# A searched instruction order, a halved first segment and LN transposes on TensorE, in a transformer block with segmented attention

## The chip, the core and the metric

The kernel runs on one core of one Trainium2 chip. The metric is device time in microseconds for one launch. The runs of one kernel spread over 1 to 1.5%, so each kernel ran several times, turn by turn with the kernel before on the same chip.

Engine names in the profile: PE is the matmul engine, PEld its weight loads (they overlap matmuls), DVE is VectorE, ACT is ScalarE, POOL is GpSimd, SP the engine that issues most DMAs.

## The reference

One transformer block on 2048 tokens of width 640, bf16: a LayerNorm, an attention in four segments of 512 tokens with 32 heads of 20, its output projection, a residual, a second LayerNorm, and a SiLU feed-forward (FFN) of width 1728. Within a segment the attention is a causal softmax; between segments it reads a memory that the earlier segments filled.

```python
q, k, v = LN(x) @ wq, LN(x) @ wk, LN(x) @ wv          # 32 heads x 20, segments of L = 512
phi = lambda t: where(t > 0, t + 1, exp(t))
M = z = 0
for s in range(4):
    p = softmax(qs @ ks.T * 20**-0.5 + causal_mask)    # within the segment
    o = g * (phi(qs) @ M) / (phi(qs) @ z + 1e-6) + (1 - g) * (p @ vs)
    M, z = M + phi(ks).T @ vs, z + sum(phi(ks))        # g = sigmoid(beta), per head
h = x + o @ wo
out = h + silu(LN(h) @ w1) @ w2
```

## The kernel before

The kernel is written as a graph of some 1,350 tasks. A task is a group of instructions for one engine: ten V matmuls of one token block, one exponential, one cast. At build time a list scheduler plays the graph through with costs in microseconds: whenever an engine is free it starts the ready task of best priority that finds its buffers free. The order that comes out is the order of the instructions on each engine. On the chip each engine works through its list in order and waits on semaphores.

```python
    def schedule(self):
        ...
        while left:
            for e in ENGS:
                if engfree[e] > now + 1e-9: continue
                best = None
                for i in cand[e]:
                    t = tasks[i]
                    if t.start is not None or t.ready > now + 1e-9: continue
                    pr = t.prio
                    if e == AC and DV in t.engs and engfree[DV] <= now + self.flex: continue
                    ...
                    if best is not None and (pr, t.idx) >= best[0]: continue
                    if not can(t): continue                # its buffers are not free
                    best = ((pr, t.idx), t)
                if best is None and e == PE and fill_ok(now):
                    ...                                    # a filler matmul on zeros
```

When PE has nothing to do and its window has been quiet, the scheduler puts in a filler: a matmul on zeros, meant to keep the granted PE clock up.

Four parts of the graph matter here.

```python
    # start: x in four loads, then wq, wk; wv waits for the LN of block 1
    for b in range(4): load_x(b, 1, -100 + b)
    load_w("q", ...); load_w("k", ...)
    load_w("wv", ..., after=lnt(1))

    # every LayerNorm ends in a DMA transpose: tokens x features -> features x tokens
    dma(f"{tag}tr{b}", [(xn, [0])], [(dstA, [i])],
        lambda e: e.dma_start_transpose(out=dst[:, :, 128*i:128*i+128], in_=xn_rot[:, xn.slot, :]), ...)

    # scores of one head group (4 heads): three tiles of key blocks over all 512 queries,
    # then the exponentials on ACT, the causal mask on POOL, P @ V on PE
    for pi, (pool, pt, js, width, cost) in enumerate((
            ("PTA", PTA, [(0, 0)], 512, ...),              # key block 0
            ("PTB", PTB, [(1, 0), (3, 384)], 512, ...),    # key blocks 1 and 3
            ("PTE", PTE, [(2, 0)], 256, ...))):            # key block 2
        ...

    # FFN of a segment: 14 row blocks over all 512 tokens
    h1: matmul(bank(ps)[0:fw, :], lhsT=w1_sb[...], rhs=hT[:, c, :])      # waits for four LN blocks
    th: th = tanh(0.5 * h1)     on ACT
    s : sT = (th + 1) * h1      on DVE
    h2: matmul over sT and w2, then x + 0.5 * h2
```

PSUM has eight banks: four for the score tiles (`sc`), four for everything else (`ps`).

The softmax here doesn't subtract the row's maximum and nothing guards it: scores larger than these inputs give would overflow.

Of the kernel before, what the change touches and what calls it, by code (L numbers as in the profile page):

```python
# [5 lines left out]
ACT = mybir.ActivationFunctionType  # L6
# [226 lines left out]
LAT = {PE: 0.125, AC: 0.16, DV: 0.14, PO: 0.09, SP: 0.0}  # L233


class Graph:
    def __init__(self, pools):
        self.pools = pools
        self.tasks = []
        self.turns = {}  # L240
        self.flex = P["flex"]
        self.filler = None
        self.fill_from = 1.0
        self.fill_to = 1e9
        self.free_order = ("x", "ps", "ex", "th", "st", "xn", "pK", "rd")
# [7 lines left out]
    def task(self, name, engs, emit, reads=(), writes=(), prio=0.0, mode=None, reserve=(), lat=None, bw=0.0):  # L253

        t = Task()
        t.name, t.engs, t.emit, t.prio, t.mode, t.lat, t.bw = name, engs, emit, prio, mode, lat, bw
# [21 lines left out]
        for a in [a for a, _ in t.reads + t.writes] + list(reserve):  # L278
            if a not in al:
                al.append(a)  # L280
# [7 lines left out]
    def schedule(self):  # L288
        import heapq
        tasks = self.tasks  # L290
        for t in tasks:
            t.succ = []
            t.npred = len(t.preds)
            t.ready = 0.0
            t.start = t.eng = None
        for t in tasks:
            for p in t.preds:
                tasks[p].succ.append(t.idx)
        free = {p: [True] * n for p, n in self.pools.items()}
        events = []  # L300
        engfree = {e: 0.0 for e in ENGS}
        pemode = [None]
        WIN = 3.4133
        busy = {}
        rate = {0: 0.5}

        def pe_rate(t):
            w = int(t / WIN)
            for v in range(max(rate), w):
                rate[v + 1] = 1.0 if busy.get(v, 0.0) >= 0.39 * WIN else 0.5  # L310
            return rate[w]

        def pe_busy(st, en, r):
            w = int(st / WIN)
            while st < en:
                e2 = min(en, (w + 1) * WIN)
                busy[w] = busy.get(w, 0.0) + (e2 - st) * r
                st = e2
                w += 1
        dmaq = [0.0]  # L320
        cand = {e: [] for e in ENGS}
        order = []
        left = len(tasks)

        def push(t):
            for e in t.engs:
                cand[e].append(t.idx)

        turn = {p: 0 for p in self.pools}

        def find(a):
            f = free[a.pool]
            if a.pool not in self.free_order and a.turn != turn[a.pool]:
                return None
            if a.size == 1:
                if a.pool == "ps":
                    n = len(f)
                    for i in range(n):
                        if f[i] and not f[i ^ 1]:
                            return i  # L340
                for i, x in enumerate(f):
                    if x:
                        return i
                return None
            for i in range(0, len(f), a.size):
                if all(f[i:i + a.size]):
                    return i
            return None

        def can(t):  # L350
            need = [a for a in t.allocs if a.slot is None]
            if not need:
                return True
            taken = []
            ok = True
            for a in need:
                i = find(a)
                if i is None:
                    ok = False
                    break  # L360
                for k in range(a.size):
                    free[a.pool][i + k] = False
                taken.append((a, i))
            for a, i in taken:
                for k in range(a.size):
                    free[a.pool][i + k] = True
            return ok

        def fill_ok(t):
            return t > self.fill_from and busy.get(int(t / WIN), 0.0) < 0.55 * WIN and t < self.fill_to  # L370

        now = 0.0
        for t in tasks:
            if t.npred == 0:
                push(t)
        done_heap = []
        rel_heap = []
        while left:
            progressed = True
            while progressed:  # L380
                progressed = False
                for e in ENGS:
                    if engfree[e] > now + 1e-9:
                        continue
                    best = None
                    for i in cand[e]:
                        t = tasks[i]
                        if t.start is not None or t.ready > now + 1e-9:
                            continue
                        pr = t.prio  # L390
                        if e == AC and DV in t.engs and engfree[DV] <= now + self.flex:
                            continue
                        if e == PE and pemode[0] is not None and t.mode != pemode[0]:
                            pr += P["mode"]
                        if best is not None and (pr, t.idx) >= best[0]:
                            continue
                        if not can(t):
                            continue
                        best = ((pr, t.idx), t)
                    if best is None and e == PE and self.filler is not None and fill_ok(now):  # L400
                        a = Alloc("ps", 1)
                        if find(a) is not None:
                            t = Task()
                            t.name, t.engs, t.prio, t.mode, t.lat, t.bw = "fill", {PE: 0.107}, 1e9, "f", None, 0.0
                            t.reads, t.writes, t.allocs, t.preds, t.succ, t.npred = [], [(a, [0])], [a], set(), [], 0
                            t.ready, t.start, t.eng = now, None, None
                            t.idx = len(tasks)
                            t.emit = self.filler(a)
                            a.users = 1
                            tasks.append(t)  # L410
                            cand[PE].append(t.idx)
                            left += 1
                            best = ((0, 0), t)
                    if best is None:
                        continue
                    t = best[1]
                    progressed = True
                    for a in t.allocs:
                        if a.slot is None:
                            i = find(a)  # L420
                            a.slot = i
                            turn[a.pool] += 1
                            for k in range(a.size):
                                free[a.pool][i + k] = False
                    cost = t.engs[e]
                    st = now
                    if e == PE and pemode[0] is not None and t.mode != pemode[0]:
                        st += 0.10
                    if e == PE:
                        pemode[0] = t.mode  # L430
                        r = pe_rate(st)
                        cost = cost / r
                        pe_busy(st, st + cost, r)
                    t.start, t.eng = st, e
                    if e == SP:

                        engfree[e] = st + cost
                        b = max(st + (0.9 if t.mode == "tr" else 0.3), dmaq[0])
                        dmaq[0] = b + t.bw
                        end = b + t.bw + 1.5  # L440
                        avail = end
                    else:
                        end = st + cost
                        engfree[e] = end
                        avail = end + (LAT[e] if t.lat is None else t.lat)
                    t.end = end
                    cand[e].remove(t.idx)
                    for e2 in t.engs:
                        if e2 != e:
                            cand[e2].remove(t.idx)  # L450
                    order.append(t)
                    left -= 1
                    heapq.heappush(done_heap, (avail, t.idx))
            nxt = [engfree[e] for e in ENGS if engfree[e] > now + 1e-9]
            nxt += [tasks[i].ready for e in ENGS for i in cand[e] if tasks[i].ready > now + 1e-9]
            if done_heap:
                nxt.append(done_heap[0][0])
# [779 lines left out]
```

## Time and profile before

| | before |
|---|---|
| median of the runs beside the changed kernel | 351.04 us (348.51 to 353.0, 4 runs) |
| profiled span | 346.4 us |
| first V matmul / first score exponential | 15.5 / 23.95 us |
| first FFN matmul | 104.4 us |
| filler matmuls | 62 before the first V matmul, 72 later |

From the profile page of before: the busy time and share of each engine, and the shares of the chain that ended last (followed back from the last instruction, at each step to what released it).

```profile
PE 320.3 (92%) x2750; PEld 165.1 (48%) x2750; DVE 239.6 (69%) x482; ACT 203.8 (59%) x258; POOL 145.5 (42%) x282
...
PE 67%; DVE 15%; ACT 7%; DMA 6%; issue 2%; SPq 1%; POOL 0%; ACTq 0%; DVEq 0%
```

PE is named first in both, but 92% busy does not mean 92% used. The Trainium skill ("Perfetto Trace Analysis", Identifying the Most-Contended Engine) says that matmul busy time is a poor measure because matmuls are pipelined. The trace agrees: a single 512-column matmul is listed at about 380 ns, yet five of them take 1.08 us in the chain, which is 2,370 columns per us. So this document counts columns: the columns of all matmuls at a round 2,400 per us. Matmuls that use a quarter of the rows or columns of the array ("row- and column-tiled") count a quarter, since four of them run side by side: sixteen of P @ V, 5,120 columns together, take 0.66 us in the chain. That gives about 256 us of real PE work in 346 us. "Density" below is this work over the time.

The chain of waits of before at the start (start in us, duration in us, what):

```profile
8.45 1.32 SPq L780
...
9.81 5.55 DMA wv_sb<-in_A_wv_dram
...
15.49 2.83 PE ps_gen L807 x10
```

SP is busy issuing a DMA transpose of the LayerNorms until 9.8 us (line 780); wv is issued after it and lands at 15.4, and only then does the first block of V matmuls start.

The first FFN matmul of before, in the view of the tile hT (count; duration min, median, max; start of the first and last in the window; forms):

```profile
L1138 PE MATMUL ps_gen<-hT,w_sb x55: 376/379/390, 104.4 to 123.0; 128*128 128x512 bf16 x55
```

It comes at 104.4 us. (The prediction says 108.4, which is only the first FFN matmul that lies on the chain.)

### The profile page before, as it was taken

To read this page: it belongs to the slowest core of one execution; us is meant where nothing else is said; L and a number is where in the kernel's file an instruction comes from. 1 tells how busy PE (TensorE), PEld (TensorE's weight loads), DVE (VectorE), ACT (ScalarE), POOL (GpSimd) and SP (SyncE) were. 2 spreads that over 40 slices of the span, in tenths; PEclk is the share of its full clock that TensorE was granted. 3 is DMA by queue.
4 is the path that set the end of the run, shared out by engine and by line. 5 is a ranking of instruction groups with operands and counts; after the bars stand their busy time and mean duration, and the time that the engine had idled before them with its cause. 6 is when DMAs were issued, how large, how long until landed. Compare 5 with 4: busy or idle time off the path is not lost.

```text
span 346.4 us, 6896 instructions
## 1 busy us (share of the span) xinstructions
PE 320.3 (92%) x2750; PEld 165.1 (48%) x2750; DVE 239.6 (69%) x482; ACT 203.8 (59%) x258; POOL 145.5 (42%) x282
## 2 busy tenths in 40 slices
PE   8499999998869999789999999999999999999996
PEld 6253445333534455345555444445554446644453
DVE  6579845699989987898666556899545782934422
ACT  1038998788568967666755788366667840014400
POOL 8606646442675545536544134547444430200000
PEclk9789999999999999999999999999999999999999
DMA  7910576549645000042136200033410004330001
GB/s 214 276 40 16 116 178 135 178 131 211 159 77 104 19 2 0 17 85 66 19 75 125 61 0 2 2 77 59 88 45 22 0 2 86 62 81 2 0 20 59
DMA packets 51552, 25.20 MB, mean 73 GB/s; under 512 B 41600, under 2 KB 50240, under 8 KB 51520
## 3 DMA queue, kind: packets, MB, share of 16 engines
q1 hardware_dynamic: 51520, 24.76, 31.7%
q8 instruction: 22, 0.36, 0.4%
q14 instruction: 10, 0.08, 0.1%
HBM read 10.33 MB, written 2.62 MB: 37 GB/s over the span
## 4 chain that ended last, share of the span: by engine, by line
PE 67%; DVE 15%; ACT 7%; DMA 6%; issue 2%; SPq 1%; POOL 0%; ACTq 0%; DVEq 0%
PE ps_gen L1166 17%; PE ps_gen L1138 16%; PE ps_gen L835 8%; PE ps_gen L807 7%; PE ps_sc L912 6%; PE ps_gen L1118 6%; PE ps_gen L955 4%; DVE QK L846 3%; ACT PTB L924 2%; ACT ex L851 2%; DMA xT<-xn_rot 2%; DVE on L1024 2%; DMA wv_sb<-in_A_wv_dram 2%; PE ps_gen L1057 2%; SPq L780 1%
## 5 line engine op out<-in xcount | busy, mean ns | idle before, releaser
L924 ACT ACTIVATE PTA<-ps_sc 128x1024 bf16<-128x1024 f32 x64 | 62.3, 1022 | 25.5 <-PE ps_sc L912 25.3
L1166 PE MATMUL ps_gen<-w_sb,sT 128*128 128x320 bf16 (+1 forms) x448 | 68.6, 300 | 2.1 <-DVE on L1024 1.4
L924 ACT ACTIVATE PTB<-ps_sc 128x1024 bf16<-128x1024 f32 x64 | 62.4, 1026 | 12.5 <-PE ps_sc L912 12.2
L1138 PE MATMUL ps_gen<-hT,w_sb 128*128 128x512 bf16 (+1 forms) x280 | 66.9, 380 | 2.4 <-DVE sT L1150 1.0
L937 POOL TENSOR_SCALAR_AFFINE_SELECT PTB<-PTB 128x512 bf16<-128x512 bf16 x64 | 41.3, 646 | 53.8 <-ACT PTB L924 51.6
L1145 ACT ACTIVATE th<-ps_gen 128x512 f32<-128x512 f32 (+1 forms) x56 | 33.2, 601 | 48.2 <-PE ps_gen L1138 46.0
L1150 DVE SCALAR_TENSOR_TENSOR sT<-th,ps_gen 128x512 bf16<-128x512 f32 (+1 forms) x56 | 37.7, 682 | 29.2 <-ACT th L1145 29.0
L1166 PEld LDWEIGHTS ps_gen<-w_sb,sT 128*128 128x128 bf16 (+1 forms) x448 | 40.1, 97 | 26.7 <-issue 8.0
L1138 PEld LDWEIGHTS ps_gen<-hT,w_sb 128*128 128x128 bf16 (+1 forms) x280 | 24.8, 98 | 34.1 <-DVE sT L1150 4.7
L937 POOL TENSOR_SCALAR_AFFINE_SELECT PTA<-PTA 128x512 bf16<-128x512 bf16 x32 | 20.6, 644 | 42.2 <-ACT PTA L924 42.1
L924 ACT ACTIVATE PTE<-ps_sc 128x1024 bf16<-128x1024 f32 (+1 forms) x40 | 33.4, 852 | 7.7 <-PE ps_sc L912 7.6
L846 DVE CAST QK<-ps_gen 128x512 bf16<-128x512 f32 x40 | 27.3, 684 | 9.9 <-ACT ex L851 8.4
L807 PE MATMUL ps_gen<-wv_sb,xT 128*128 128x320 bf16 x160 | 25.6, 310 | 5.9 <-DMA wv_sb<-in_A_wv_dram 5.1
L1176 DVE SCALAR_TENSOR_TENSOR x_tok<-ps_gen,x_tok 128x640 bf16<-128x640 f32 x16 | 13.2, 824 | 25.6 <-PE ps_gen L1166 25.6
L851 ACT ACTIVATE ex<-ps_gen 128x512 bf16<-128x512 f32 x30 | 17.7, 598 | 20.9 <-PE ps_gen L835 13.9
L757 DVE BATCH_NORM_STATS2 stt<-x_tok 128x6 f32<-128x320 bf16 x64 | 27.9, 478 | 2.2 <-DMA x_tok<-in_A_x_dram 2.1
L912 PE MATMUL ps_sc<-QK 20*128 20x512 bf16 (+3 forms) x320 | 25.4, 302 | 3.3 <-ACT PTE L924 1.3
L971 DVE TENSOR_SCALAR oTs<-ps_gen,lsc 128x512 bf16<-128x512 f32 x31 | 23.0, 743 | 7.0 <-PE ps_gen L955 6.9
L835 PE MATMUL ps_gen<-xT,wqr 128*128 128x512 bf16 x100 | 25.7, 389 | 1.7 <-ACT ex L851 1.5
L1032 POOL TENSOR_TENSOR otok<-on 128x320 bf16<-128x320 bf16 x24 | 19.3, 804 | 18.6 <-DVE on L1024 15.0
L835 PE MATMUL ps_gen<-xT,wkr 128*128 128x512 bf16 x100 | 25.0, 380 | 1.7 <-DVE QK L846 1.7
L937 POOL TENSOR_SCALAR_AFFINE_SELECT PTE<-PTE 128x512 bf16<-128x512 bf16 x32 | 20.9, 652 | 10.4 <-ACT PTE L924 9.7
(69 smaller groups left out, 404.9 us busy)
## 6 DMA issues: line engine op xcount, KB each, us to landing
out_dram<-x_tok SPq DMA_DIRECT2D x16, 160.0 KB, 1.8
w_sb<-in_B_w_dram SPq DMA_DIRECT2D x5, 432.0 KB, 4.2
x_tok<-in_A_x_dram SPq DMA_DIRECT2D x3, 640.0 KB, 5.4
w_sb<-in_B_w_dram SPq DMA_DIRECT2D x3, 640.0 KB, 4.9
QKV<-QK SPq DMA_DIRECT2D x16, 72.0 KB
sT<-in_A_wq_dram SPq DMA_DIRECT2D x1, 800.0 KB, 6.6
sT<-in_A_wk_dram SPq DMA_DIRECT2D x1, 800.0 KB, 8.3
wv_sb<-in_A_wv_dram SPq DMA_DIRECT2D x1, 800.0 KB, 5.5
```

What stands on the lines that cost most here:

```text
L757: T.add(DV, lambda e, hh=hh: e.bn_stats(out=stt[:, s, 6 * hh:6 * hh + 6], in_=xb[:, 320 * hh:320 * hh + 320]), reads=R((xa, xsub)), writes ...
L807: fns.append(lambda e, c=c, hh=hh: e.matmul(bank(ps, hh)[:, 0:320], lhsT=xT[:, c, 128 * i:128 * i + 128], rhs=wv_sb[:, c, 320 * hh:320 * h ...
L835: fns = [lambda e, kc=kc: e.matmul(bank(ps), lhsT=wt[:, kc, c, :], rhs=xT[:, kc, :], start=(kc == 0), stop=(kc == NC - 1)) for kc in range ...
L846: (lambda e: e.tensor_copy(out=o, in_=bank(ps)))
L851: T.add(AC, lambda e: e.activation(out=ex[:, exa.slot, :], in_=bank(ps), func=ACT.Exp), reads=R((ps, [0])), writes=R((exa, [0])))
L912: fns.append(lambda e, j=j, o=o, n=n, r=r: e.matmul(sc_all[:, o:o + n], lhsT=ka[32 * r:32 * r + DH, 128 * j:128 * j + 128], rhs=qa[32 * r: ...
L924: T.add(AC, lambda e: e.activation(out=pt[:, pta.slot, q0:q0 + nq, :], in_=sc3[:, b0:b0 + nq, 0:width], func=ACT.Exp, scale=SCALE), reads= ...
L937: fns.append(lambda e, v=v: e.affine_select(out=v, in_=v, pattern=[[0, 4], [1, 128]], compare_op=ALU.is_ge, fill=0.0, base=0, channel_mult ...
L1138: fns = [lambda e, c=c: e.matmul(bank(ps)[0:fw, :], lhsT=w1_sb[:, c, 128 * f:128 * f + fw], rhs=hT[:, c, :], start=(c == 0), stop=(c == NC ...
L1145: T.add(AC, lambda e: e.activation(out=th[0:fw, tha.slot, :], in_=bank(ps)[0:fw, :], func=ACT.Tanh, scale=0.5), reads=R((ps, [0])), writes ...
L1150: T.add(DV, lambda e: e.scalar_tensor_tensor(out=sT[0:fw, f, :], in0=th[0:fw, tha.slot, :], scalar=1.0, in1=bank(ps)[0:fw, :], op0=ALU.add ...
L1166: fns.append(lambda e, f=f, fw=fw, hh=hh: e.matmul(bank(ps, hh)[:, 0:320], lhsT=sT[0:fw, f, 128 * i:128 * i + 128], rhs=w2_sb[0:fw, f, 320 ...
```

## The change

Its intent: stop deciding the order at build time. An offline search found a fixed order, an engine and a buffer slot for each task, and the kernel replays it. The graph itself changes too:

1. The first four LN transposes are matmuls against an identity on TensorE, copied out of PSUM by ACT or DVE. wv is loaded at once.
2. Segment 0 is computed in two query halves, and so are its output projection and the first FFN layer, so that the FFN can begin when the first two token blocks are done.
3. In segments 1 to 3 the small score tile (key block 2) is shared by two head groups.
4. x has 12 block slots instead of 16; the copies that gather the last three head groups (QKV) take 12 DMAs per segment instead of 16.
5. The copies that rearrange wq and wk after loading are cut by blocks of columns and may run on ACT as well as DVE, and a Q or K projection waits only for its own block. Before, all five copies of a weight ran on DVE and every projection waited for all of them.

```diff
     def schedule(self):
-        import heapq
-        ...                                   # the list scheduler, 190 lines
+        todo = {t.name: t for t in self.tasks}
+        owner = {p: [None] * n for p, n in self.pools.items()}
+        order = []
+        for row in ORDER:
+            name, _, slots = row.partition(":")
+            name, _, eng = name.partition("/")
+            ...
+            t = todo.pop(name)
+            assert not any(self.tasks[p].name in todo for p in t.preds), name
+            t.eng = {"A": AC, "D": DV, "G": PO}[eng] if eng else list(t.engs)[0]
+            ...                               # take the slots, check that they are free
+            order.append(t)
+ORDER = """
+zpad:0 x0:0 mt0 mt1 mt3 mta3 iota halfc epsc x1:1 x3:2 sel n1_st0:0 w_wv:0 n1_st1:1 n1_rs0 n1_ap0:0 fill31:0
+n1_tp0:0 n1_rs1 n1_ap1:1 x2:3 fill5:2 n1_tp1:2 n1_te0/A:0 n1_st3:0 n1_rs3 n1_st2:1 n1_te1/A epsg0 n1_rs2 w_q:0 v00:0
+...                                           # 1,389 rows in all
@@ LayerNorm
+        if tag == "n1_" and b < 4:
+            def e_tp(eng):
+                fns = [lambda e, c=c: e.matmul(ps_all[:, ...128 * c...], lhsT=xn_rot[:, xn.slot, 128*c:128*c+128],
+                                               rhs=ident[:, :], start=True, stop=True) for c in range(NC)]
+            ...                               # and a copy PSUM -> xT on ACT or DVE
+            return
         dma(f"{tag}tr{b}", ...)
@@ scores
+        if s == 0:
+            for g in range(NG):               # queries 0 to 255
+                pe = scores(f"{g}x", "PTE", PTE, [(g, 0, 0, 256, 0), (g, 1, 128, 256, 256)], k, 384)
+                tick(g, k, f"{g}x", 0, 2, ...)
+            for g in range(NG):               # queries 256 to 511
+                pa = scores(f"{g}ya", "PTA", PTA, [(g, 0, 256, 512, 0), (g, 1, 256, 512, 256)], k)
+                pb = scores(f"{g}yb", "PTB", PTB, [(g, 2, 256, 512, 0), (g, 3, 384, 512, 256)], k + P["qkp"], 384)
+                tick(g, k, f"{g}y", 2, 4, ...)
+        else:
+            ...
+                if g % 2 == 0:                # key block 2 of two head groups in one tile
+                    pe = scores(f"{k}e", "PTE", PTE, [(g, 2, 256, L, 0), (g + 1, 2, 256, L, 256)], ...)
@@ FFN
+        parts = [(0, 2), (2, 4)] if s == 0 else [(0, 4)]
@@ pools
-        "x": NB, ...
+        "x": 12, ...
```

## The prediction

> **What bounds it now.** The busy table has PE at 92% of 346.4 us, DVE 69%, ACT 59%. The Trainium skill ("Perfetto Trace Analysis", Identifying the Most-Contended Engine) says matmul busy time misjudges PE, and this trace agrees: weight loads are busy 48%, and in the chain of waits a block of five 512-column matmuls takes 1.08 us, about 2370 columns per us, although each is listed at 380 ns. Counting columns so (row- and column-tiled matmuls at a quarter), PE has about 258 us of work. By windows it streams:
> - 0 to 24 us: 6 us. First real matmul 15.49 us (62 fillers before), first score exponential 23.95 us.
> - 24 to 73 us, segment 0: two thirds dense. ACT binds: its timeline is almost gapless, 5 us of exponentials per head group.
> - 73 to 120 us: 0.7 dense. The chain goes output projection, DVE, mask, transposes; the first FFN matmul starts at 108.4 us, because it needs all four blocks of segment 0. 33 of the 72 later fillers lie in 80 to 120 us.
> - 120 to 280 us: 0.85 dense, DVE busy 11 to 19 of each 20 us.
> - 280 to 346 us: the last segment's projection and FFN, 0.82 dense, ACT nearly idle.
>
> **What the change does.**
> 1. Start. wv loads fourth, without a wait (before: issued 9.81, landed 15.4). The first four transposes go to PE: 20 matmuls of 128 columns and four copies of about 0.8 us, instead of DMA transposes that take 2.9 us to land. The skill ("TensorE: Matmul & The Clock Gate", PE-mode transpose) warns of the copy; here it sits on idle ACT and DVE. First V matmul at about 8 us (estimate: 1.3 MB at 250 KB/us plus 2.5 us); q weights near 11.5, k weights near 14.5; first score exponential about 18 us. Worth 6 us.
> 2. Segment 0 in halves. Same exponential elements, same PE columns; adds about 12 PSUM reads of 0.4 us on DVE and 14 tanh. Blocks 0 and 1 finish early, so output projection and half of the FFN can fill PE while ACT binds and blocks 2 and 3 normalise. Worth 12 us: 87 to 120 holds 22 us of columns, and fillers after the start fall from 72 to 4.
> 3. Order. Nine QK, six V and five output casts move from DVE to ACT: DVE about 230 instead of 240 us busy, ACT about 230 instead of 204. Middle density 0.85 to 0.88: 5 us.
> 4. Paired small blocks: same exponentials in segments 1 to 3, fewer handoffs of all four score banks; 1 us. QKV copies 16 to 12 per segment: off the path. x in 12 slots: only room.
> 5. Tail: same work, about 60 us after the last exponential; at most 2 us.
>
> Sum: about 26 us, all on the critical path because PE or ACT is the limit there. The timed median is 1.4% over the profiled span.
>
> **Predicted: 324 us, 311 to 338 eight times in ten.** Faster by over 2%: 0.94; within 2%: 0.05; slower: 0.01.
>
> **What would show it.** First V matmul at 7 to 10 us; first score exponential at 17 to 20; segment 0's last one at 64 to 70 instead of 73; first FFN matmul before 65 instead of 108; density in 24 to 120 above 0.75; last exponential to end near 61 us, as now.
>
> **What would make it wrong.** ACT, at about 93% between 18 us and the tail, becomes the limit and the order leaves it gaps (near 335); the fixed order waits for DMA transposes that land later than its search assumed; weights land late behind the x loads; or the search packs the middle better than 0.88 (near 312).

## More of the kernel before

Windows of before: start and end in us, length, then for each engine the busy time and the number of instructions, then the granted PE clock (1.00 is full), the DMA share and GB/s.

```profile
core 0: us, PE busy (x) PEld busy (x) DVE busy (x) ACT busy (x) POOL busy (x), PEclk, DMA share, GB/s
8.00:16.00 8.00, 2.87 (x25) 2.18 (x24) 4.86 (x17) 0.35 (x2) 5.87 (x29) 0.80 1.16 269
16.00:24.00 8.00, 8.00 (x40) 3.98 (x39) 4.61 (x10) 0.65 (x2) 1.49 (x7) 0.78 0.26 84
24.00:60.00 36.00, 34.22 (x319) 15.74 (x317) 25.78 (x55) 32.03 (x41) 19.60 (x34) 1.00 0.49 111
...
80.00:100.00 20.00, 16.74 (x184) 8.96 (x181) 18.64 (x43) 14.40 (x17) 11.54 (x22) 1.00 0.73 146
100.00:120.00 20.00, 17.69 (x167) 8.53 (x167) 18.74 (x44) 15.84 (x21) 11.70 (x23) 1.00 0.39 71
```

The clock is 0.80 and 0.78 in the first two windows. From 24 to 60 us ACT is busy 32 of 36 us: the exponentials of segment 0. From 80 to 120 us DVE is busy 18.6 and 18.7 of each 20 us.

The end of before, from its chain of waits:

```profile
325.25 0.70 DVE sT L1150
...
325.99 2.46 PE ps_gen L1138 x10
...
329.92 12.21 PE ps_gen L1166 x84
```

Here PE waits in turn for tanh on ACT and the product on DVE: h1 has two PSUM banks, because the first h2 block already holds the other two.

## The result, and the profile after

Ratios here are the mean time of one kernel's fast runs over that of the other's fast runs of the same rounds, so they are not quite the ratio of the medians that stand beside them. Executions over 1.5% slower than the fastest of the same kernel are left out of the means.

| | before | after |
|---|---|---|
| median | 351.04 us (4 runs) | 332.01 us (330.56 to 333.4, 4 runs) |
| ratio | 1 | 0.9502, 95% interval 0.944 to 0.9564 |
| profiled span | 346.4 us | 330.1 us |
| first V matmul / first score exponential | 15.5 / 23.95 | 9.2 / 19.3 us |
| first FFN matmul | 104.4 | 65.5 us |
| first FFN matmul of segment 3 to the end | 37.9 | 34.5 us |

The changed kernel is about 19 us faster: inside the predicted range, 8 us above the predicted time. The same two lines of its page:

```profile
PE 307.5 (93%) x2874; PEld 166.9 (51%) x2874; DVE 230.8 (70%) x504; ACT 219.6 (67%) x306; POOL 144.6 (44%) x282
...
PE 56%; DVE 23%; ACT 7%; DMA 5%; SPq 5%; issue 3%; POOL 1%; DVEq 0%; ACTq 0%
```

DVE has 9 us less work and ACT 16 us more, since casts moved; DVE is where the prediction had it (230), ACT is 10 us under its 230. Less of the chain is PE and more of it is DVE. The chain of waits of after at the start, then the first V matmuls in the view of the tile wv_sb:

```profile
2.65 6.80 DMA x_tok<-in_A_x_dram
...
13.03 0.74 DVE xT L744
...
13.81 1.53 PE ps_gen L776 x10
```

```profile
L776 PE MATMUL ps_gen<-wv_sb,xT x30: 296/299/310, 9.2 to 15.0; 128*128 128x320 bf16 x30
```

V starts at 9.2 us and a block of ten takes 1.53 us instead of 2.83. Windows of after, in the same columns as those of before:

```profile
8.00:16.00 8.00, 5.80 (x44) 3.92 (x45) 5.56 (x16) 5.16 (x13) 2.73 (x8) 1.00 0.78 270
16.00:24.00 8.00, 7.29 (x40) 2.98 (x38) 7.40 (x19) 4.35 (x11) 3.55 (x10) 1.00 0.00 0
24.00:60.00 36.00, 32.63 (x366) 15.99 (x367) 24.98 (x64) 29.20 (x39) 18.84 (x36) 0.95 0.55 138
...
80.00:100.00 20.00, 18.71 (x187) 11.16 (x188) 18.20 (x45) 18.09 (x26) 14.48 (x37) 1.00 0.55 113
100.00:120.00 20.00, 16.66 (x208) 9.51 (x209) 18.41 (x39) 16.60 (x24) 13.92 (x22) 1.00 0.54 124
```

The clock is 1.00 from the first V matmul on, with a dip somewhere in 24 to 60 us. From 80 to 120 us DVE is nearly full, as it was. The first FFN matmuls of after, and a piece of its chain near 106 us:

```profile
L1129 PE MATMUL ps_gen<-hT,w_sb x115: 269/273/297, 65.5 to 122.2; 128*128 128x256 bf16 x105, 128*64 128x256 bf16 x10
```

```profile
105.63 0.82 DVE on L989
106.45 0.66 DVE oTs L938
107.11 0.33 DVE sT L1143
...
108.41 0.82 DVE on L989
```

The FFN starts 39 us earlier than before. From 80 to 120 us PE now does 29.3 us of columns instead of 25.4, still far from the 40 that would fill it: between 91 and 115 us 18.7 us of the chain are DVE, one instruction after another (normalising the attention output, its eviction, the FFN product, LN). The end of after, from its chain of waits:

```profile
287.45 8.09 PE ps_gen L1160 x56
295.55 15.44 PE ps_gen L1129 x70
310.99 15.96 PE ps_gen L1160 x112
```

All 70 h1 matmuls come in one run, then all 112 of h2: the order releases the banks of h2_11 and h2_10 first and gives h1 four banks.

How far the real PE work had come, in us of columns of the matmuls begun by then, fillers left out (after contains 1.1 us for the 20 transposes). The last row says how much earlier after had done the same work as before at that time, transposes left out:

| time, us | 24 | 40 | 60 | 80 | 100 | 120 | 200 | 280 | end |
|---|---|---|---|---|---|---|---|---|---|
| before | 6.3 | 18.7 | 28.8 | 42.9 | 54.0 | 68.3 | 133.7 | 201.5 | 255.6 |
| after | 12.7 | 21.0 | 33.7 | 46.8 | 63.0 | 76.1 | 142.6 | 212.9 | 256.6 |
| after is earlier by | 6.4 | 3.6 | 4.9 | 4.3 | 8.8 | 9.8 | 8.7 | 11.1 | 16.3 |

The lead of 6.4 us at 24 us is partly spent at 40 us, comes back to about 9 at 100 to 200, and reaches 11 at 280 and 16 at the end. So the whole of segment 0 gave about 3 us, not 12. The loss is early: from 24 to 40 us after does 8.3 us of columns, before 12.4. The chain of after leads there through something that the prediction had put "off the path", the copies that gather QKV:

```profile
30.31 0.64 SPq L841
...
35.74 2.34 DMA QKV<-QK
...
38.13 0.36 PE ps_sc L877 x4
...
40.80 2.49 PE ps_gen L776 x10
```

From 30.2 to 38.1 us the chain is SP issuing these copies (line 841) one after another, some 0.65 us each, with one transpose between, and the landing of the last. No run tested what they cost. What the trace can't tell is which of the edits and the order earned the gain. That needed runs.

### The profile page after: what moved, and what is told of

Read it like the earlier page. It is cut to its first block, busy times and chain, and to the rows that moved or that the text cites. A ratio compares the mean times of both kernels' runs of the same rounds, so it can differ in the third digit from the quotient of the medians.

```text
span 330.1 us, 7228 instructions
## 1 busy us (share of the span) xinstructions
PE 307.5 (93%) x2874; PEld 166.9 (51%) x2874; DVE 230.8 (70%) x504; ACT 219.6 (67%) x306; POOL 144.6 (44%) x282
## 4 chain that ended last, share of the span: by engine, by line
PE 56%; DVE 23%; ACT 7%; DMA 5%; SPq 5%; issue 3%; POOL 1%; DVEq 0%; ACTq 0%
PE ps_gen L1160 18%; PE ps_gen L1129 13%; PE ps_gen L804 6%; PE ps_sc L877 4%; PE ps_gen L923 4%; DVE stt L708 4%; PE ps_gen L1105 4%; DMA x_tok<-in_A_x_dram 4%; PE ps_gen L776 3%; DVE on L989 3%; DVE QK L815 2%; SPq L841 2%; ACT PTA L888 2%; ACT ex L820 2%; PE ps_gen L952 2%
## 5 line engine op out<-in xcount | busy, mean ns | idle before, releaser
L888 ACT ACTIVATE PTA<-ps_sc 128x1024 bf16<-128x1024 f32 x64 | 62.9, 1025 | 13.4 <-PE ps_sc L877 12.4
L1129 PE MATMUL ps_gen<-hT,w_sb 128*128 128x512 bf16 (+3 forms) x350 | 68.4, 338 | 2.5 <-DVE Vx L787 0.7
L1160 PE MATMUL ps_gen<-w_sb,sT 128*128 128x320 bf16 x448 | 67.3, 300 | 0.6 <-DVE QK L815 0.2
L888 ACT ACTIVATE PTB<-ps_sc 128x1024 bf16<-128x1024 f32 (+1 forms) x64 | 59.9, 978 | 8.0 <-PE ps_sc L877 6.4
L1137 ACT ACTIVATE th<-ps_gen 128x512 f32<-128x512 f32 (+3 forms) x70 | 35.1, 520 | 39.6 <-PE ps_gen L1129 34.4
L1160 PEld LDWEIGHTS ps_gen<-w_sb,sT 128*128 128x128 bf16 x448 | 40.5, 98 | 24.1 <-issue 7.2
L1143 DVE SCALAR_TENSOR_TENSOR sT<-th,ps_gen 128x512 bf16<-128x512 f32 (+3 forms) x70 | 38.7, 570 | 16.4 <-ACT th L1137 15.9
L1129 PEld LDWEIGHTS ps_gen<-hT,w_sb 128*128 128x128 bf16 (+1 forms) x350 | 31.4, 98 | 31.7 <-issue 3.0
L815 DVE CAST QK<-ps_gen 128x512 bf16<-128x512 f32 x31 | 21.0, 684 | 12.6 <-ACT ex L820 7.1
L1105 PE MATMUL ps_gen<-wo_sb,oT 128*128 128x320 bf16 x160 | 23.9, 299 | 3.5 <-DVE Mz L1070 1.2
L877 PE MATMUL ps_sc<-QK 20*128 20x256 bf16 (+3 forms) x360 | 24.1, 285 | 2.2 <-DVE QK L815 1.0
L938 DVE TENSOR_SCALAR oTs<-ps_gen,lsc 128x512 bf16<-128x512 f32 (+1 forms) x34 | 21.3, 628 | 6.8 <-PE ps_gen L923 6.8
```

The costliest lines, as they stand in the source:

```text
L815: (lambda e: e.tensor_copy(out=o, in_=bank(ps)))
L877: fns.append(lambda e, j=j, o=o, r=r, q0=q0, q1=q1, qa=qa, ka=ka: e.matmul(sc_all[:, o:o + q1 - q0], lhsT=ka[32 * r:32 * r + DH, 128 * j:1 ...
L888: T.add(AC, lambda e: e.activation(out=pt[:, pta.slot, q0:q0 + 2, 0:width], in_=sc3[:, b0:b0 + 2, 0:width], func=ACT.Exp, scale=SCALE), re ...
L1105: fns.append(lambda e, c=c, hh=hh: e.matmul(bank(ps, hh)[:, 0:320], lhsT=oT[:, c, 128 * i:128 * i + 128], rhs=wo_sb[:, c, 320 * hh:320 * h ...
L1129: fns = [lambda e, c=c: e.matmul(bank(ps)[0:fw, lo:hi], lhsT=w1_sb[:, c, 128 * f:128 * f + fw], rhs=hT[:, c, lo:hi], start=(c == 0), stop= ...
L1137: T.add(AC, lambda e: e.activation(out=th[0:fw, tha.slot, lo:hi], in_=bank(ps)[0:fw, lo:hi], func=ACT.Tanh, scale=0.5), reads=R((ps, [0])) ...
```

## The experiments

All kernels below gave correct results. Theories: **O**, most of the gain is the searched order; **S**, it is the structure (halves, transposes, pairs), and any sensible order would do. Later a third one stood out: neither part is worth much without the other.

### e1_list: the changed structure under the old list scheduler

```diff
-        for row in ORDER: ...
+        ...                                   # the list scheduler of before, its priorities as before
```

> The changed structure (halves of segment 0, transposes on TensorE, paired score blocks, 12 x slots, early wv) but with the greedy list scheduler of the kernel before in place of the fixed order. Theory O, most of the 19 us comes from the searched order (sequence and choice of engine), says 342 to 352 us. Rival S, most comes from the new structure and any reasonable order harvests it (this is what my prediction's terms 1 and 2, 18 us of 26, said), says 330 to 338 us.

Measured: 362.9 us (361.07 to 364.47), ratio 1.0358 (1.0304 to 1.0412). Both theories missed. The same tasks that take 332 us in the searched order are 3.6% slower than before when the old scheduler orders them. Its priorities had been set for the old structure, which is probably part of the reason; no run tuned them for the new one.

### e5_listfull: as e1_list, with segment 0 in full query blocks

```diff
-        if s == 0:                            # two halves
+        if s == 0:                            # key blocks 0, 1+3, 2 over all 512 queries, as before
-        parts = [(0, 2), (2, 4)] if s == 0 else [(0, 4)]
+        parts = [(0, 4)]
```

> As e1_list, the old list scheduler, but with segment 0 put back to full ticks of 512 queries (projection, FFN and weight loads of segment 0 as before); early wv, TensorE transposes, paired blocks and 12 x slots stay. The difference from e1_list is the halving alone under one scheduler. The prediction said 12 us for the halving and 6 us for the start: then this one is at 343 to 346 us and e1_list some 10 us lower. If halving by itself is worth little, e1_list and this one differ by less than 3 us.

Measured: 352.76 us, ratio 1.007 (1.0003 to 1.0136). Both expectations missed: under the list scheduler the halves cost 10 us. And the transposes on PE, the early wv and the pairs, all still in it, gain nothing: its first score exponential comes at 20.7 us instead of 23.95, and the 3 us are gone by the end.

### e4_tail: the changed kernel with the old order in the last stretch

```diff
-... n2_tr13 h1_3_6_0:0 h1_3_4_0:1 th3_4_0:0 s3_4_0:0 h1_3_1_0:2 ... h1_3_10_0:3 ... h2_14_0:2 ...
+... n2_tr13 h1_3_0_0:0 h1_3_1_0:1 th3_0_0:0 s3_0_0:0 ... h2_12_0:2 th3_5_0:1 s3_5_0 h1_3_6_0:0 ...
```

> The changed kernel with one piece of its order undone: the last stretch (14 first-FFN blocks of segment 3 and the second FFN of blocks 12 to 15) in the order of the kernel before, which interleaves the second FFN of block 12, holding two of the four accumulator banks, with the first FFN. The trace says this stretch took 37.9 us before and 34.5 after, from its first FFN matmul to the end. Theory: the order there is worth 3 to 3.5 us, so 335 to 336 us. Rival, that the tail is only shifted and its length is set by the work: 332 us.

Measured: 334.66 us, ratio 0.9558 (0.952 to 0.9595). The control of the next call (the changed kernel itself) was 0.9451, and e2_fill below, in the same call, 331.11 us. So the order of the last stretch is worth about 3 us, a little under what was expected.

### e2_fill: 32 more fillers at 31 to 40 us

```diff
-... mtb3 fill2:1 ... e4x2:1 fill2:1 ...
+... fill4:1 av0x:0 ... mtb3 fill6:1 ... mk1x fill4:1 ... fill6:1 ... fill6:1 ... fill6:0 ... fill4:2
```

> The changed kernel with 32 more filler matmuls of 256 columns spread over PE's order where it ran at 31 to 40 us in the trace. There the granted clock fell to 0.50 between 38.6 and 43 us (kernel before: 72 fillers after the start, clock 1.00 throughout). Theory: the missing fillers cost 1.5 to 2.5 us, so 329.5 to 330.5 us, with a granted clock of 1.00 in that stretch. Rival, that the stretch waits for exponentials and QKV copies and not for PE: clock back at 1.00, time unchanged or up to 1 us longer.

The granted clock of after in two windows of 2 us, where it fell:

```profile
38.00:40.00 2.00, 1.36 (x20) 0.69 (x24) 1.79 (x6) 1.68 (x3) 1.77 (x4) 0.86 0.58 117
40.00:42.00 2.00, 2.00 (x17) 0.86 (x10) 0.93 (x3) 1.59 (x3) 1.55 (x2) 0.50 0.53 113
```

The same windows of e2_fill, then pieces of its chain (line 609 is the fillers, line 775 a block of V):

```profile
38.00:40.00 2.00, 1.53 (x25) 0.70 (x23) 1.38 (x4) 1.65 (x3) 1.91 (x4) 1.00 0.66 130
40.00:42.00 2.00, 2.00 (x26) 1.11 (x25) 1.93 (x5) 1.29 (x3) 1.27 (x2) 1.00 0.48 104
```

```profile
33.13 0.83 PE ps_gen L609 x6
...
34.49 0.65 PE ps_gen L609 x6
...
41.29 1.47 PE ps_gen L775 x10
```

Measured: 331.11 us, ratio 0.9455 (0.9418 to 0.9492), beside 0.9451 of the control. The clock is full again and the time does not move, as the rival said. Its reason is not shown, though: the V block on the chain takes 1.47 us here instead of the 2.49 of after, but 4.7 us of fillers stand on the same chain between 29 and 41 us. So either PE would have waited there anyway, or the fillers cost what the clock saves. A run that kept the clock up without taking PE's time would tell; none was made.

### a_ctl, e3_dmatr and e6_pool

a_ctl is the changed kernel unchanged, a control.

> The changed kernel itself, as a control for the others of this call: 332 us, ratio to the kernel before 0.945 to 0.95. In the earlier call its last stretch in the old order gave 334.7 us and the added fillers 331.1 us.

Measured: 331.23 us, ratio 0.9451 (0.9406 to 0.9497).

e3_dmatr undoes only the transposes on PE, the rest of the order kept:

```diff
-        if tag == "n1_" and b < 4:
+        if False:
-n1_tp0 ... n1_te0/A ... n1_tp1 ... n1_te1/A ... n1_tp3 n1_tp2 ...
+w_q w_k n1_tr0 n1_tr1 ... n1_tr3 ... n1_tr2 ...
```

> The changed kernel with one part undone: the first four LN transposes are DMA transposes again, issued behind the loads of the q and k weights as in the kernel before; the rest of the order is kept. Theory: the start is on the critical path and DMA transposes land 3 us after issue behind the weight loads, so the first V matmul moves from 9.2 us to about 11 to 12 us and the whole is 3 to 5 us longer, 335 to 337 us. Rival, that exponentials bind segment 0 anyway and a later start is absorbed (as e5_listfull, with an early start and no gain, hints): at most 1 us longer.

Measured: 339.21 us, ratio 0.9671 (0.963 to 0.9712): 7.7 to 8 us slower than the control, more than expected. Its chain of waits at the start:

```profile
2.66 5.50 DMA x_tok<-in_A_x_dram
8.17 5.90 DMA xT<-xn_rot
...
17.84 4.22 DMA x_tok<-in_A_x_dram
```

The transposes of blocks 0 and 1, issued at 5.7 and 8.2 us among the loads of x and the weights, land at 13.5 and 14.1 us, 7.8 and 5.9 us after their issue where 3 us were expected, and the first V matmul starts at 13.6 us instead of 9.2. There is a second cost: SP issues its DMAs in order and waits for each LN before it can issue that block's transpose. So the load of the next four x blocks, which stands behind them, is issued at 17.8 us and lands at 22.05; in the changed kernel it is issued at 7.2 us. The kept order makes this worse: it lets the LNs of blocks 3 and 2 reuse the buffers of blocks 1 and 0, so they wait until 14.1 us for those slow transposes. Part of the 8 us may thus be the price of an order made for fast transposes; f4_dmaln below has an order of its own.

e6_pool moves the set-up work of POOL to the start, to see whether POOL slows DVE at 80 to 120 us:

```diff
+... vpad0 mt2 mta0 mta1 mta2 mtb0 ... mm0 ... mm11 re_wq3/D ...     # were spread over 30 to 110 us
```

> The changed kernel with the constants that POOL builds at 82 to 104 us in its order (12 mask copies, 12 small multiplies and their selects, some 6 us) moved to POOL's idle time at 13 to 18 and 26 to 28 us. In the stretch of 80 to 120 us DVE is busy 18.3 of each 20 us, its phi operations with two SBUF inputs take 0.59 to 0.68 us there against 0.43 where POOL is idle, and POOL lies on the chain of waits at 97 to 99 us. Theory: POOL's moved work slows DVE there, and moving it back gains 1 to 2 us (330 to 331). Rival: POOL and DVE do not limit that stretch or the masks alone keep POOL in the way: within 0.5 us of the control.

Measured: 331.97 us, ratio 0.9452 (0.9406 to 0.9499): no gain. The suspicion came from the Trainium skill ("GPSIMD Engine Reference", Specifications), which says that POOL shares its SBUF interfaces with VectorE, with contention for DVE instructions with two SBUF inputs among others. The trace of after does show such a DVE product of two SBUF tiles (phi) at 0.43 us when alone and up to 0.90 us with POOL busy; but taking this POOL work out of the stretch brought nothing to the end. It did not test the contention itself: the slowest phi products of the stretch lie at 109 to 115 us, beside POOL's masks and multiplies, which stayed there, and they are as slow in e6 (up to 0.90 us).

### f1_oldstruct, f2_fullticks, f3_halves: our own searched orders

To part order and structure, we wrote a search of our own. It gives each task a priority of its own, plays the list scheduler, changes priorities at random and keeps what shortens the schedule in a simple cost model. Its output is a fixed order, replayed as the changed kernel does. The same search was given three structures, one order for each, so how much one search differs from the next is not known.

```diff
 # f1_oldstruct: the graph of before, untouched; only the replay and
+ORDER = """ zpad:0 iota x2:0 mt3 x0:1 sel vpad1 x3:2 x1:3 fill62:1 mt1 beta ... """
 # f2_fullticks: the changed graph, segment 0 in full query blocks (the edit of e5_listfull)
+ORDER = """ zpad:0 mt3 x0:0 epsc fill31:0 x2:1 halfc vpad1 x1:2 w_k:0 ... """
 # f3_halves: the changed graph, untouched
+ORDER = """ zpad:0 vpad1 x0:0 fill31:0 x1:1 x2:2 mt2 mt1 x3:3 vpad0 beta ... """
```

> The kernel before, task for task (LN transposes by DMA, full query blocks in segment 0, unpaired small score blocks, x in 16 slots), but its instructions are in a fixed order that an offline search of ours found for exactly this structure, as the changed kernel's order was found for the changed one. Only the order and the buffer slots differ from before. Theory O (most of the gain of 19 us is the searched order, and the structure only adds some): 333 to 341 us, ratio 0.95 to 0.972. Theory S (the order serves to make the new structure usable, the old one has little to win): at least 345 us, ratio over 0.985. Our search puts it about 15 units of its own model below the order of before, and the model's differences between kernels have so far come out on the chip at about 0.7 to 1.1 of their size, so I lean to O with 337.

Measured: 351.57 us, ratio 1.0044 (0.999 to 1.0099). Theory O falls in its plain form, and the number is theory S's: a searched order on the old structure gained nothing, although our model had promised 15. Two reserves. f3 below shows our search to be some 10 us poorer than the one that made the change, so a better order of the old structure is not ruled out. And the fillers of f1 are all at the start, and its clock was 0.91 from 24 to 60 us, 0.96 from 60 to 100 and 0.97 from 100 to 200, where before had 1.00. If all of that clock mattered, it would be an estimated 8 us (36 x 0.09 + 40 x 0.04 + 100 x 0.03).

> The changed structure (LN transposes on TensorE, paired small blocks, x in 12 slots), but segment 0 in full query blocks again, in an order that our search found for this structure. Theory H (halving segment 0 is a needed part of the gain): at least 337 us, ratio over 0.962. Theory N (with a searched order the halving is worth nothing): 328 to 334 us, ratio 0.936 to 0.954, level with the changed kernel, though its first FFN matmul comes late, well after 90 us. Our search's model has it level with the changed kernel, so I lean to N. Earlier the same structure under the list scheduler gave 352.8.

Measured: 339.01 us, ratio 0.9696 (0.9653 to 0.9739). By its numbers this is theory H's outcome, and the lean to N missed: 7 to 8 us worse than the changed kernel, 12.6 better than f1. But f3, next, has the halves and an order of the same search and is no better, so the distance to the changed kernel can't be put down to the halves. Its first FFN matmuls:

```profile
L1119 PE MATMUL ps_gen<-hT,w_sb x20: 379/379/403, 108.0 to 114.8; 128*128 128x512 bf16 x15, 128*64 128x512 bf16 x5
```

So f2 wins 11 us over before with an FFN that starts at 108 us, later than before's 104.

> The changed structure with its halves, in an order of our own search: a control of the search. If our search is as good as the one that made the changed kernel, 329 to 334 us (ratio 0.94 to 0.954). Its model has it 4 units above the changed kernel's order, so about 334 to 337 is more likely; the list scheduler gave 362.9 for the same instructions. If it comes out over 345, our search's orders don't carry over to the chip, and the other two runs of this call say less.

Measured: 341.75 us, ratio 0.9781 (0.9731 to 0.9832): 21 us better than the list scheduler on the same graph, 10 us worse than the order that came with the change (334 to 337 us had been expected), and 2.7 us worse than f2. So our search is the poorer one, and at equal search the halves did not pay.

### f4_dmaln: f2_fullticks with the LN transposes by DMA

```diff
-        if tag == "n1_" and b < 4:
+        if False:
 # and a searched order of its own
+ORDER = """ zpad:0 iota x2:0 vpad0 sel beta x1:1 halfc x3:2 vpad1 fill62:1 w_k:0 ... """
```

> As f2_fullticks (changed structure, full query blocks in segment 0, our own search), but with all LN transposes by DMA as before, and an order that the same search found anew for this structure. Left against f1_oldstruct: paired small score blocks and x in 12 slots. f2 was 0.970, f1 1.004, so 12.6 us lie between them. Theory T (the four LN transposes on TensorE carry the larger part): at least 346 us, ratio over 0.985. Theory P (pairs and the freed buffers carry it): at most 342 us, ratio under 0.978. Undoing the transposes inside the shipped order cost 7.7 us, so I lean to T with 347.

Measured: 347.5 us (344.73 to 349.39), ratio 0.9914 (0.9866 to 0.9963). Theory T holds: the transposes carry 8.5 of the 12.6 us between f1 and f2 (by the ratios, since the calls differ, 7.6 of 12.2). The remaining 4 us belong to the pairs, the early wv, the freed buffers, the fewer QKV copies and the weight copies by blocks together. From the chain of f4:

```profile
6.73 9.91 DMA xT<-xn_rot
...
16.68 2.85 PE ps_gen L768 x10
```

The first V matmul waits until 16.7 us, and a block of ten takes 2.85 us. Windows of f4, then of f2:

```profile
0.00:24.00 24.00, 15.84 (x86) 10.06 (x87) 17.51 (x56) 6.72 (x15) 16.43 (x67) 0.86 0.70 185
24.00:60.00 36.00, 32.98 (x262) 14.77 (x261) 18.32 (x35) 26.77 (x35) 13.42 (x22) 0.81 0.41 91
60.00:100.00 40.00, 32.21 (x280) 14.32 (x279) 27.89 (x65) 30.17 (x41) 17.28 (x30) 0.87 0.67 144
```

```profile
0.00:24.00 24.00, 18.14 (x123) 10.53 (x125) 17.48 (x55) 12.30 (x22) 15.10 (x63) 1.00 0.53 170
24.00:60.00 36.00, 31.96 (x286) 14.40 (x290) 19.69 (x43) 28.30 (x37) 18.18 (x32) 0.86 0.52 104
60.00:100.00 40.00, 33.65 (x348) 16.49 (x348) 36.30 (x84) 34.82 (x47) 22.56 (x40) 1.00 0.68 154
```

With DMA transposes PE has done less in the first 100 us (47.9 us of columns against at least 57.1; some matmul records of f2 are missing) and has a lower clock in each of these windows. How much of the 8.5 us goes through the clock was not separated: no run of f4 with more fillers was made.

### c1: the best pieces together

```diff
-... n1_st0:0 w_wv:0 n1_st1:1 ... n1_ap1:1 x2:3 fill5:2 ...
+... n1_st0:0 x2:3 w_wv:0 n1_st1:1 ... n1_ap1:1 fill5:2 ...
 # with the fillers of e2_fill and the early POOL work of e6_pool
```

> The changed kernel with three edits together: 32 fillers at 31 to 40 us, the Pool constants issued at the start, and the load of the third x block ahead of the wv load. The first two alone gave 0.9455 and 0.9452 beside a control of 0.9451, so what is new is the load. If the start is on the critical path: the third block's LN and its share of Q come about 1 us earlier, 0.940 to 0.944. If a microsecond of start is lost before the end: 0.944 to 0.947. I expect the latter with 0.944.

Measured: 331.77 us, ratio 0.9481 (0.9445 to 0.9518). No gain over the changed kernel, and a little above both ranges named. No version of these runs beats the change clear of noise.

## Why the prediction was right or wrong

**The total.** 324 us was predicted, 332.01 came: right in direction, in range, 8 us too low. The gain was 19 us instead of 27. Under that, the terms were off and partly cancelled; that the number still lies in the range is partly luck.

**Start, 6 us.** Right about the events: first V matmul at 9.2 us (7 to 10 predicted), first score exponential at 19.3 (17 to 20). Its worth at 24 us fits (6.4 us of lead); to the end it was undersized: undoing the transposes costs 7.7 us in the shipped order and about 8 in orders of our own search. The skill's warning ("TensorE: Matmul & The Clock Gate", PE-mode transpose) that the result has to be copied out of PSUM holds: one of the four copies, 0.74 us on DVE, stands on the chain of after, where the prediction had them all on idle engines. The prediction took 2.9 us for a DMA transpose to land, the median of all 16 of that kind; the first four, among the weight loads, took 5.3 to 6.4. It also left out that the DMA transposes hold up the issue of the next x blocks (e3), and that PE, having had to wait, then runs V at a lower clock (2.83 instead of 1.53 us per block).

**Segment 0 in halves, 12 us.** This is the step that failed: "Blocks 0 and 1 finish early, so output projection and half of the FFN can fill PE while ACT binds". The first half is what the trace shows: the first FFN matmul came at 65.5 us instead of 104.4, close to the "before 65" of the prediction, and fillers after the start fell from 72 to 4. The conclusion is not. The density from 24 to 120 us is 0.66 against 0.65 before, where above 0.75 was predicted, and the lead grew from 6.4 us to about 9 by 120 to 200 us: some 3 us for everything that changed in segment 0, instead of 12. At equal search the halves are 2.7 us slower than full blocks (f3 against f2), under the list scheduler 10 us slower (e1 against e5), and f2 gains 11 us with its first FFN matmul at 108 us.

The prediction said that segment 0's last exponential would come at 64 to 70 us; in the changed kernel's trace it came at about 74, as before, because the exponentials started earlier but had more gaps: ACT is busy 29.2 of the 36 us from 24 to 60, against 32.0. And the time that the early FFN could fill was partly lost before: from 24 to 40 us PE did a third less than before, with the QKV copies on the chain. At 80 to 120 us the early FFN did fill PE somewhat (29.3 us of columns instead of 25.4); there DVE holds it back, at 18.2 and 18.4 of 20 us and with most of the chain from 91 to 115 us. Filling PE with work whose product DVE must make helps little when DVE is full. That is my reading of the trace of after; no run took DVE work away there, and it is not the general reason. In f3_halves, where the halves lose too, DVE has room in these windows, and from 100 to 120 us 12.8 us of the chain are PE:

```profile
80.00:100.00 20.00, 17.84 (x213) 10.67 (x215) 14.93 (x43) 18.58 (x30) 9.42 (x19) 1.00 0.49 100
100.00:120.00 20.00, 18.06 (x198) 10.38 (x198) 14.64 (x31) 14.34 (x20) 10.72 (x18) 0.91 0.26 54
```

So why the halves cost time in f3 and e1 stays open. Whether they pay in an order as good as the shipped one is open too, since no such order of full blocks was to be had.

**Order, 5 us.** Not a term that can be added. In the middle, from 120 to 280 us, after does 136.8 us of columns and before 133.2: some 4 us more, near what was predicted. But on the same graph the list scheduler takes 362.9, our search 341.75, the shipped order 332: the order, with its engines and fillers, is worth 31 us once the structure is there. On the old structure our search gained nothing (351.57), and the new structure without halves gained nothing under the old scheduler (352.76). In these runs the gain needs both. A likely reason, not shown, is that the old scheduler's priorities and the old start fit each other, and what the new start frees has to be handed on through 300 us of waits; e5, which loses its 3 us on the way, would fit that.

**Pairs, 1 us.** With the early wv, the buffers, the QKV copies and the weight copies: about 4 us (f1 against f4), with the reserves told at f1. What the pairs alone are worth was not measured. The QKV copies were called "off the path"; in after they stand on the chain from 30.2 to 38.1 us.

**Tail, at most 2 us.** About 3 us (e4), by the order there, which has four banks for h1 instead of two. The trace agrees: 34.5 instead of 37.9 us from its first FFN matmul. From the last exponential to the end it is 58.8 us instead of 68.2; the prediction said about 60.

**What would have made it wrong.** The prediction named "ACT becomes the limit and the order leaves it gaps (near 335)". That is nearest to what came, with DVE rather than ACT on the chain from 91 to 115 us.

## What to carry to other kernels

When a change brings a new structure and a new order together, don't add up what each is worth: here each alone gave nothing or less, in the orders that we could make, and together 19 us. To judge the structure, give old and new the same effort of ordering and compare those. Before counting on early work to fill an idle engine, look at what that stretch waits for, and at which engine the work needs next. And a DMA that stands at the head of everything can be worth replacing by a few matmuls if PE is idle anyway: here about 8 us.

## What the Trainium skill lacked or had wrong

- "TensorE: Matmul & The Clock Gate" (Part 1) puts the fall of the clock to an idle window of about 3.4 us. In the changed kernel the clock fell to 0.50 at 40 to 42 us although PE is listed busy 1.36 to 2.00 us of every 2 us from 28 to 40 us; what was low was the density, about 8 us of columns in the 16 us from 24 to 40. Part 1 also tells of a kernel whose clock swung with short idle gaps between groups of matmuls, which is nearer, but it gives no density below which the clock is lost.
- The same page (Part 4: PE-mode transpose) gives about 275 ns for a 128x128 transpose in a kernel and says that transpose mode does not raise the clock. Here the transposes are plain matmuls against an identity: 219 ns each, with the granted clock at 1.00 in their window. Whether they or the 36 fillers around them kept it there was not separated.
- "DMA: Bandwidth & Descriptors" (DMA Transpose) gives constraints, but not how long one small transpose takes beside other loads. Here those of 128x640 took a median of 2.6 us from issue to landing in a quieter stretch (segment 1 of the changed kernel), 5.6 us among the first loads (before) and up to 9.9 us there (f4_dmaln).
